# Linear attention with a routed MoE: token numbers written into the masks of ranks, and the third expert slot chosen during attention

## The chip, the cores and the metric

The kernel runs on one core of a Trainium2 chip. The metric is the device time of one execution in microseconds (us); the runs' median is the kernel's time. Engines are named as the profile names them: PE is TensorE (PEld its weight loads), DVE is VectorE, ACT is ScalarE, POOL is GpSimd, SP is SyncE.

## The reference

Attention with 8 batches, 8 heads, 576 positions and 64 dimensions per head is followed by a mixture of 8 experts over the 4608 resulting rows of 512 numbers. Cut to what matters:

```python
def phi(x):
    proj = np.einsum('bhsd,df->bhsf', x, w_phi)
    proj = proj - np.max(np.abs(proj), axis=-1, keepdims=True)
    return np.concatenate([np.exp(proj), np.exp(-proj)], axis=-1)
q_p, k_p = (phi(q), phi(k))
kv = np.einsum('bhsf,bhsd->bhfd', k_p, v)
z = np.sum(k_p, axis=2)
num = np.einsum('bhsf,bhfd->bhsd', q_p, kv)
den = np.einsum('bhsf,bhf->bhs', q_p, z)[..., None] + 1e-06
x = (num / den).transpose(0, 2, 1, 3).reshape(B * S, H * D)

do_compute = x @ w_skip > 0
out = x.copy()
xc = x[do_compute]
logits = xc @ w_gate
e_idx = np.argmax(logits, axis=1)
probs = softmax(logits); gate_w = probs[np.arange(len(xc)), e_idx]
for e in range(E):
    mask = e_idx == e
    h = np.maximum(xc[mask] @ w1[e], 0.0)
    y[mask] = gate_w[mask, None] * (h @ w2[e])
out[do_compute] = xc + y
```

So each row goes to one expert or to none, and which rows an expert gets is known only on the chip.

## The kernel before

**Attention** runs in a software pipeline over some 90 iterations. Each handles a piece of a k unit and of a q unit (4 heads of one batch): transposed load (L298), projection on PE (L321), maximum and subtraction on DVE (L328, L331), exponentials on ACT, the sums z of k on POOL (L354 to L360), products on PE (L389, L487), the normalization by 1/den on DVE (`norm`, L434). PSUM tiles come from `bank(tag)`; during attention tag O has two buffers, shared by the products, the ranks and the choices. From iteration 8 to 78 PE's instructions stand in the order of the code; before and after that a scheduler orders them, as it orders the other engines all through attention.

**Ranks.** When a batch of rows is done, `post(b)` picks each row's expert (`OH`, a one-hot row per token in 36 tiles of 128 tokens) and queues three functions for some iterations later. `rank` counts each token's rank within its expert. It splits the rank: `RKH` is the rank divided by 128, and `OP` holds for each tile a mask of 128 x 128, which is 1 where the token's rank modulo 128 equals the column (L607). The masks are made on POOL, one instruction per tile, and for the last batch on DVE. `index` multiplies the mask by a right-hand side that holds the token's number, so that PE sorts token numbers into rank order. A number over 256 isn't exact in bf16, so it goes in two parts (`ids`, L171): a multiple of 128, and the rest plus one; hence two matmuls per tile (L630), each with `rhs`, the one-hot of the higher rank times one part (L619).

**Choices.** The two fullest experts are chosen after batch 5 (`pick(0)`, `pick(1)`), so that their first 256 rows can be gathered early (slots E). `pick_third` (L942) chooses a third slot in the same way from the counts of 27 tiles: one matmul, then 17 small DVE instructions that depend on one another. It is called in step 2 of the MoE part (`at(TAB[0], pick_third)`, L1182).

**The MoE part** is a list of steps. Each step multiplies one weight chunk of 512 KB (a quarter of w1 or w2 of an expert) with the rows of a slot: 8 steps for each slot E, C and D. Weights are read by SP's queue, cut by `split` (L193) into a high part (ACT, L198) and a low part (DVE in one instruction, or POOL in four, L203, for chunks 0, 1, 2, 4, 6, 8, 9, 11, 12, 14, 17, 19, 21 of the first slots). `rows` turns gathered rows (PE), and cuts them in the same way (ACT L785, DVE L786). The results are scattered to the output by POOL's queue (L855) with an index that DVE makes (`si`, L854).

Beside the first 17 steps stands the making of the **tables** for the other slots: `rests[0]`, the rank of the last batch (step 4, masks on DVE), and then the generator `tables()`, a piece in each of the steps of `CFG['tab']`. Its last big pieces compare each token's place with all 62 columns (`eq`, L1057), multiply by the two parts of the token's number (`rx`, L1060), four groups of 9 tiles in four steps, and then sum all of them with 72 matmuls (L1068). In the MoE part every engine works in the order of the code.

`xrows` keeps the rows in DRAM for the gathers. Batch rows are stored there so that a partition's four tiles are four consecutive rows (`rowm`, L241).

Of the kernel before, what the change touches and what calls it, by code (L numbers as in the profile page):

```python
# [8 lines left out]
F32 = mybir.dt.float32  # L9
# [15 lines left out]
def kernel(  # L25
# [93 lines left out]
    pad0 = const.tile([P, 3, 2], I32, name="pad0")  # L119
    mark = const.tile([1, 32], I32, name="mark")[:, 0:1]  # L120
# [21 lines left out]
    def setup():  # L142
        nc.gpsimd.memset(ones_b, 1.0)
        nc.gpsimd.memset(ones_f, 1.0)
        nc.gpsimd.memset(Stot, 0.0)
        nc.gpsimd.affine_select(
            out=tri, in_=ones_b, pattern=[[1, P]], base=-1, channel_multiplier=-1,
            compare_op=ALU.is_ge, fill=0.0,
        )
        nc.gpsimd.iota(iota_p, pattern=[[1, P]], base=0, channel_multiplier=0, allow_small_or_imprecise_dtypes=True)  # L150
        nc.gpsimd.iota(desc, pattern=[[-1, E]], base=E, channel_multiplier=0, allow_small_or_imprecise_dtypes=True)
        nc.gpsimd.memset(ones_b, 1.0)
        NB2 = B // 2
# [14 lines left out]
        nc.vector.tensor_copy(out=sid, in_=kt_i[:, 1])  # L168
# [60 lines left out]

    with actx:  # L230
# [10 lines left out]
        rowm = [xr[b // 2, b % 2 * 512:b % 2 * 512 + 512].rearrange("(p g) m -> p g m", g=4) for b in range(B)]  # L241
# [273 lines left out]
        def post(b):  # L515
# [63 lines left out]
            rhs = sm("rhs", [5, 2, nsh], BF16)  # L579

            def rank():
# [24 lines left out]
                for t in range(nt):  # L606
                    (nc.vector if last else nc.gpsimd).tensor_scalar(  # L607
                        out=OP[:, t0 + t, :], in0=iota_p, scalar1=rkp[:, t:t + 1], scalar2=None, op0=ALU.is_equal)
# [5 lines left out]
                for s in range(S):  # L614
# [4 lines left out]
                nc.gpsimd.tensor_tensor(  # L619
                    out=rhs[:, 0:nt],  # L620
                    in0=rm4[:, 0:nt].rearrange("p t (o e) s -> p t o (e s)", o=1).broadcast_to([P, nt, 2, nsh]),
                    in1=ids[:, T].rearrange("p t (c o) -> p t c o", o=1).broadcast_to([P, nt, 2, nsh]), op=ALU.mult)

            def index():
# [3 lines left out]
                for t in range(nt):  # L628
                    for c in range(2):
                        nc.tensor.matmul(  # L630
                            ix, OP[:, t0 + t, :], rhs[:, t, c, :], start=(t == 0 and c == 0),
# [310 lines left out]
    def pick_third():  # L942


        cs = bank("K")[:, 0:NTE * E]
        nc.tensor.matmul(cs, ones_b, OH[:, 0:NTE, :].rearrange("p t e -> p (t e)"), start=True, stop=True)
        n = const.tile([P, E], F32, name="n_e")
        d = const.tile([P, E], F32, name="d_e")
        mx = const.tile([P, 2], F32, name="mx_e")
        nc.vector.tensor_reduce(out=n, in_=cs.rearrange("p (t e) -> p e t", e=E), axis=AX.X, op=ALU.add)  # L950
        for j in range(2):
            nc.vector.scalar_tensor_tensor(out=d, in0=n, scalar=float(SLOT), in1=pks[:, j], op0=ALU.min, op1=ALU.mult)
            nc.vector.tensor_tensor(out=n, in0=n, in1=d, op=ALU.subtract)
        nc.vector.tensor_tensor(out=d, in0=n, in1=pks[:, 1], op=ALU.mult)
        nc.vector.tensor_tensor(out=n, in0=n, in1=d, op=ALU.subtract)
        nc.vector.tensor_reduce(out=mx[:, 0:1], in_=n, axis=AX.X, op=ALU.max)
        nc.vector.scalar_tensor_tensor(out=d, in0=n, scalar=mx[:, 0:1], in1=desc, op0=ALU.is_equal, op1=ALU.mult)
        nc.vector.tensor_reduce(out=mx[:, 1:2], in_=d, axis=AX.X, op=ALU.max)
        nc.vector.tensor_scalar(out=d, in0=d, scalar1=mx[:, 1:2], scalar2=None, op0=ALU.is_equal)
        nc.vector.tensor_scalar(  # L960
            out=eid0[:, 2:3], in0=mx[0:1, 1:2], scalar1=-1.0, scalar2=float(E), op0=ALU.mult, op1=ALU.add)
        nc.vector.scalar_tensor_tensor(out=pks[:, 2], in0=n, scalar=float(SLOT), in1=d, op0=ALU.is_ge, op1=ALU.mult)
        tp = const.tile([P, 2, E], F32, name="tp_e")
        ea = const.tile([P, 2], F32, name="ea_e")
        nc.vector.tensor_tensor(
            out=tp.rearrange("p s e -> p e s"), in0=acc.rearrange("p (e s) -> p e s", s=2),
            in1=pks[:, 2].rearrange("p (e o) -> p e o", o=1).broadcast_to([P, E, 2]), op=ALU.mult)
        nc.vector.tensor_reduce(out=ea, in_=tp, axis=AX.X, op=ALU.add)
        places(idg0[:, 2], pad0[:, 2], ea)

    def tables():
        i34 = const.tile([P, NCOL], F32, name="i34")
        nc.gpsimd.iota(i34, pattern=[[1, NCOL]], base=1, channel_multiplier=0, allow_small_or_imprecise_dtypes=True)
# [77 lines left out]
        rxs = []  # L1051
        for g, t0 in enumerate(range(0, NT, C)):
            eq = mo.tile([P, 2, P + 64], F32, tag="hsum", name="eq")
            eq = eq.rearrange("p a n -> p (a n)").bitcast(BF16)[:, 0:C * NCOL].rearrange("p (t c) -> p t c", c=NCOL)
            rx = mo.tile([P, C, 2, NCOL], BF16, tag="rx", name="rx", bufs=4)
# [4 lines left out]
            nc.vector.tensor_tensor(  # L1060
                out=rx, in0=eq.rearrange("p t (o c) -> p t o c", o=1).broadcast_to([P, C, 2, NCOL]),
# [236 lines left out]
```

## Time and profile before

| | us |
|---|---|
| median of 3 runs | 623.17 |
| lowest and highest | 622.90, 623.51 |
| the profiled execution | 620.68 |
| its span | 619.0 |

The mean granted clock of PE in the profiled execution is 0.982. The page's chain of waits covers only the last microseconds, so the places where PE waits are read from the waits, the timelines and the tables of stages instead. In a timeline a row has its start, its length, the engine, the line, the operation, output<-input and how many were merged, then in brackets the idle time before it and what ended it.

### The profile page before, as it was taken

The page shows a single profiled execution, that of the slowest core. Times are in us where ns is not written, and L with a number is a line of the kernel's source. Part 1 is how long each engine was busy: PE and PEld are TensorE (multiplying, and loading weights), DVE is VectorE, ACT ScalarE, POOL GpSimd, SP SyncE. Part 2 cuts the span into 40 slices and gives each one's busy share as a digit, 9 for nine tenths or more (in the row PEclk, how much of TensorE's full clock was granted, in tenths as well). Part 3 has the DMA queues.
Part 4 walks back from the last instruction along what each step waited for, and adds up shares of the span by engine and source line. Part 5 has one row for each costly group of instructions (what it writes and reads, how often), then busy time and mean ns, then how long its engine had stood idle before and what let it go on. Part 6 is the DMA issues. An engine that isn't in the chain of part 4 may idle for free. (4 is left out here: it accounts for less than half of the span.)

```text
span 619.0 us, 18767 instructions
## 1 busy us (share of the span) xinstructions
PE 570.2 (92%) x7486; PEld 468.9 (76%) x7486; DVE 512.0 (83%) x1084; ACT 330.4 (53%) x649; POOL 360.5 (58%) x390
## 2 busy tenths in 40 slices
PE   4699999999999999999999898699999898999993
PEld 2477777777777677776777788598888787989892
DVE  5899999999989999999986699957688887956851
ACT  3466556456656556556446445324658554665630
POOL 5665565564744747456661657974468855559121
PEclk9999999999999999999999898979999899999998
DMA  9988888887667766423152789676767678597200
GB/s 157 161 140 162 185 184 177 192 188 139 144 151 158 162 131 143 123 70 102 37 191 94 209 302 309 221 249 182 223 225 248 233 248 290 182 314 237 88 19 29
DMA packets 250233, 108.33 MB, mean 175 GB/s; under 512 B 192417, under 2 KB 235553, under 8 KB 250144
## 3 DMA queue, kind: packets, MB, share of 16 engines
q1 hardware_dynamic: 245632, 97.58, 60.9%
q0 software_dynamic: 3200, 9.45, 4.4%
q8 instruction: 60, 0.98, 0.6%
q10 hardware_dynamic: 1312, 0.08, 0.1%
q14 instruction: 29, 0.24, 0.1%
HBM read 83.86 MB, written 24.02 MB: 174 GB/s over the span
## 5 line engine op out<-in xcount | busy, mean ns | idle before, releaser
L203 POOL TENSOR_TENSOR w<-wraw_c,w 128x256 fp32r<-128x256 f32 x124 | 114.6, 958 | 51.1 <-ACT w L198 51.1
L354 POOL TENSOR_TENSOR z<-ek 128x512 f32<-128x512 f32 x64 | 81.5, 1273 | 98.4 <-ACT ek L347 73.6
L198 ACT ACTIVATE w<-wraw_c 128x1024 fp32r<-128x1024 f32 x96 | 97.5, 1051 | 4.3 <-DMA wraw_c<-in_moe_w_dram 2.9
L203 DVE TENSOR_TENSOR w<-wraw_c,w 128x1024 fp32r<-128x1024 f32 x65 | 86.9, 1345 | 12.9 <-ACT w L198 10.7
L328 DVE TENSOR_REDUCE m<-ps_P 128x8 f32<-128x1024 f32 (+2 forms) x86 | 88.6, 1030 | 6.4 <-PE ps_P L321 6.2
L331 DVE TENSOR_TENSOR u<-ps_P,m 128x1024 f32<-128x1024 f32 (+2 forms) x86 | 88.8, 1033 | 3.1 <-DVE xTt L296 0.2
L321 PE MATMUL ps_P<-wsrc,xT 64*64 64x128 f32 x2048 | 77.9, 281 | 12.1 <-DVE xT L298 6.9
L487 PEld LDWEIGHTS ps_O<-kva,eq 128*64 128x64 f32 x2048 | 74.5, 136 | 16.5 <-issue 5.7
L487 PE MATMUL ps_O<-kva,eq 128*64 128x74 f32 x2048 | 77.6, 228 | 4.1 <-DVE lgm L450 4.0
L321 PEld LDWEIGHTS ps_P<-wsrc,xT 64*64 64x64 f32 x2048 | 56.7, 134 | 27.4 <-issue 18.4
L373 ACT ACTIVATE eq<-ps_U 128x512 f32<-128x512 f32 x64 | 37.9, 592 | 64.7 <-PE ps_U L367 64.2
L389 PE MATMUL ps_K<-ek,v 128*64 128x256 f32 x512 | 70.8, 394 | 0.0
L855 POOL DMA_INDIRECT out_dram<-o,si x22 | 28.8, 1310 | 63.9 <-DVE si L854 56.8
L922 PE MATMUL ps_O<-w,hh 128*128 128x512 f32 x160 | 64.2, 401 | 0.0
L346 ACT ACTIVATE ek<-u 128x512 f32<-128x512 f32 x64 | 40.4, 631 | 38.4 <-DVE u L331 23.0
L367 PE MATMUL ps_U<-ident,u 128*128 128x128 f32 x288 | 49.1, 287 | 2.5 <-DVE u L331 1.9
L298 DVE STREAM_TRANSPOSE xT<-raw 128x512 f32<-128x512 f32 x64 | 44.8, 702 | 5.8 <-PE ps_P L321 2.8
L926 PE MATMUL ps_O<-w,hh 128*128 128x512 f32 x120 | 47.3, 394 | 1.3 <-POOL w L203 1.3
L389 PEld LDWEIGHTS ps_K<-ek,v 128*64 128x64 f32 x512 | 31.9, 137 | 20.9 <-issue 11.3
L927 PE MATMUL ps_O<-w,hlo 128*128 128x512 f32 x120 | 47.2, 393 | 0.0
L909 PE MATMUL ps_P<-x,w 128*128 128x256 f32 x144 | 38.9, 299 | 4.7 <-DVE x L786 4.7
L358 POOL TENSOR_TENSOR z<-z 128x512 f32<-128x512 f32 x32 | 40.8, 1275 | 2.5
(259 smaller groups left out, 1206.6 us busy)
## 6 DMA issues: line engine op xcount, KB each, us to landing
wraw_c<-in_moe_w_dram SPq DMA_DIRECT2D x96, 512.0 KB, 4.0
raw<-in_k_dram SPq DMA_DIRECT2D x64, 144.0 KB, 3.3
raw<-in_q_dram SPq DMA_DIRECT2D x64, 144.0 KB, 4.4
v<-in_v_dram SPq DMA_DIRECT2D x64, 128.0 KB, 2.8
out_dram<-xm SPq DMA_DIRECT2D x16, 512.0 KB, 4.2
xrows<-xm SPq DMA_DIRECT2D x8, 516.0 KB, 4.3
xrows<-xm SPq DMA_DIRECT2D x8, 512.0 KB, 4.7
vt<-in_v_dram SPq DMA_DIRECT2D x32, 32.0 KB, 2.8
```

What stands on the lines that cost most here:

```text
L198: nc.scalar.activation(out=hi, in_=raw, func=AF.Copy)
L203: eng.tensor_tensor(out=lo[:, r], in0=raw[:, r], in1=hi[:, r].bitcast(F32), op=ALU.subtract)
L321: nc.tensor.matmul(p[s * 64:s * 64 + 64, hd, (nj + j) * NF:(nj + j + 1) * NF], xT[r, g * P + s * 64:g * P + s * 64 + 64], wsrc[r], start=T ...
L328: nc.vector.tensor_reduce(out=m.rearrange("p (j h) -> p j h", h=2), in_=pv, axis=AX.X, op=ALU.max, apply_absolute_value=True)
L331: nc.vector.tensor_tensor(out=uu[:, 0:2 * nj, :].rearrange("p (j h) f -> p j h f", h=2), in0=pv, in1=m.rearrange("p (j h o) -> p j h o", h ...
L354: zeng.tensor_tensor(out=z, in0=e[:, 0:2, :], in1=e[:, 2:4, :], op=ALU.add)
L367: nc.tensor.transpose(t[:, tt * P:(tt + 1) * P], uu[:, tt, :], ident)
L389: nc.tensor.matmul(o[hd * 64:hd * 64 + 64, :], u.v[:, 2 * hd + pr, g * D:(g + 1) * D], u.e[i][:, 2 * j + hd, :], start=(g == 0), stop=False,)
L487: nc.tensor.matmul(ov[s * 64:s * 64 + 64, 2 * j + hd, :], e[:, half, j, hd, s * 64:s * 64 + 64], kva[:, half, 2 * pr + hd, :], start=(half ...
L922: nc.tensor.matmul(y[sub], hh[:, t], wh[:, fi, :], start=first, stop=False)
L926: nc.tensor.matmul(y[sub], hh[:, t], wl[:, fi, :], start=False, stop=False)
L927: nc.tensor.matmul(y[sub], hlo[:, t], wh[:, fi, :], start=False, stop=last)
```

## The change

It moves the token numbers from the right-hand sides into the masks. Each mask of ranks is made twice, as `OP[:, t, 0]` with 128 t and as `OP[:, t, 1]` with p + 1 in place of the 1 (one instruction with a comparison and a multiplication each). The right-hand sides are then the plain one-hots `rm4` and `eq`; the products `rhs` and `rx` and the tile `ids` are gone. For a number to be 128 t + p, `rowm` now puts token p of a tile in row p of 128 consecutive ones. The comparisons of the tables keep their tiles until the 72 matmuls, which stand together behind the last comparison, in the step where they stood. `pick_third` is called in attention, five iterations after `rest` of batch 5; its matmul takes a buffer of tag O.

```diff
-    ids = const.tile([P, NT, 2], BF16, name="ids")
+    wcol = const.tile([P, NT + 1], I32, name="wcol")
-    OP = const.tile([P, NT, P], BF16, name="OP")
+    OP = const.tile([P, NT, 2, P], BF16, name="OP")
...
+        nc.gpsimd.iota(wcol[:, 0:NT], pattern=[[P, NT]], base=0, channel_multiplier=0)
+        nc.gpsimd.iota(wcol[:, NT:NT + 1], pattern=[[1, 1]], base=1, channel_multiplier=1)
...
-        nc.vector.tensor_scalar(out=h_i[:, 1], in0=kt_i[:, 0], scalar1=127, scalar2=None, op0=ALU.bitwise_and)
-        nc.vector.tensor_tensor(out=h_i[:, 0], in0=kt_i[:, 0], in1=h_i[:, 1], op=ALU.subtract)
-        nc.vector.tensor_scalar(out=h_i[:, 1], in0=h_i[:, 1], scalar1=1.0, scalar2=None, op0=ALU.add)
...
-        nc.vector.tensor_copy(out=ids.rearrange("p t c -> p c t"), in_=h_i)
...
+    def pick_third():
+        cs = bank("O")[:, 0:NTE * E]
...
-        rowm = [xr[b // 2, b % 2 * 512:b % 2 * 512 + 512].rearrange("(p g) m -> p g m", g=4) for b in range(B)]
+        rowm = [xr[b // 2, b % 2 * 512:b % 2 * 512 + 512].rearrange("(g p) m -> p g m", p=P) for b in range(B)]
...
-                for t in range(nt):
-                    (nc.vector if last else nc.gpsimd).tensor_scalar(
-                        out=OP[:, t0 + t, :], in0=iota_p, scalar1=rkp[:, t:t + 1], scalar2=None, op0=ALU.is_equal)
+                for c in range(2):
+                    for t in range(nt):
+                        (nc.vector if last else nc.gpsimd).tensor_scalar(
+                            out=OP[:, t0 + t, c, :], in0=iota_p, scalar1=rkp[:, t:t + 1],
+                            scalar2=wcol[:, NT:NT + 1] if c else wcol[:, t0 + t:t0 + t + 1], op0=ALU.is_equal, op1=ALU.mult)
...
-                nc.gpsimd.tensor_tensor(
-                    out=rhs[:, 0:nt],
...
-                            ix, OP[:, t0 + t, :], rhs[:, t, c, :], start=(t == 0 and c == 0),
+                            ix, OP[:, t0 + t, c, :], rm4[:, t].rearrange("p e s -> p (e s)"), start=(t == 0 and c == 0),
...
+                    later.append((now[0] + CFG["post"][2] + 5, pick_third))
...
-    def pick_third():
-        cs = bank("K")[:, 0:NTE * E]
...
+        def found():
+            t0, eq = rxs.pop(0)
+            for t in range(C):
+                for c in range(2):
+                    nc.tensor.matmul(
+                        ix, OP[:, t0 + t, c, :], eq[:, t, :], start=(t0 + t == 0 and c == 0),
+                        stop=(t0 + t == NT - 1 and c == 1))
+
         for g, t0 in enumerate(range(0, NT, C)):
-            eq = mo.tile([P, 2, P + 64], F32, tag="hsum", name="eq")
-            rx = mo.tile([P, C, 2, NCOL], BF16, tag="rx", name="rx", bufs=4)
+            if g % 2:
+                eq = mo.tile([P, C, NCOL], BF16, tag="rx", name="eq", bufs=2)
+            else:
+                eq = mo.tile([P, 2, P + 64], F32, tag="hsum", name="eq")
...
-            nc.vector.tensor_tensor(
-                out=rx, in0=eq.rearrange("p t (o c) -> p t o c", o=1).broadcast_to([P, C, 2, NCOL]),
-                in1=ids[:, T].rearrange("p t (c o) -> p t c o", o=1).broadcast_to([P, C, 2, NCOL]), op=ALU.mult)
-            rxs.append((t0, rx))
+            rxs.append((t0, eq))
             yield
-        for t0, rx in rxs:
...
+        while rxs:
+            found()
...
-    at(TAB[0], pick_third)
```

Lines of the changed kernel have other numbers: the masks are L633 there, the comparisons L1061, the choice L231 to L253 with L222 and L223.

Where instructions stand, engine by engine, at three places. First DVE at the end of attention, where the normalization of a q piece (`xm`, `lgm`) follows that of the pieces `xt`, `lgt`. Before:

```order
L331 TENSOR_TENSOR u<-ps_P,m 128x512
L438 TENSOR_SCALAR den<-ps_O 128x4
L442 RECIPROCAL rec<-den 128x4
L449 TENSOR_TENSOR xt<-ps_O,rec 128x2x2x64
L450 TENSOR_TENSOR lgt<-ps_O,rec 128x36
L438 TENSOR_SCALAR den<-ps_O 128x4
L442 RECIPROCAL rec<-den 128x4
L449 TENSOR_TENSOR xm<-ps_O,rec 128x4x64
L450 TENSOR_TENSOR lgm<-ps_O,rec 128x2x18
L328 TENSOR_REDUCE m<-ps_P 128x2
```

Now, the last part of the choice and what follows it:

```order
L243 TENSOR_REDUCE mx_e<-d_e 128x1
L244 TENSOR_SCALAR d_e<-d_e,mx_e 128x8
L245 TENSOR_SCALAR eid_125<-mx_e 1x1
L247 SCALAR_TENSOR_TENSOR pks<-n_e,d_e 128x8
L250 TENSOR_TENSOR tp_e<-acc,pks 128x8x2
L253 TENSOR_REDUCE ea_e<-tp_e 128x2
L464 TENSOR_SCALAR den<-ps_O 128x4
L222 TENSOR_SCALAR idg_126<-ea_e 128x2
L223 TENSOR_SCALAR pad_127<-ea_e 128x2
L468 RECIPROCAL rec<-den 128x4
L475 TENSOR_TENSOR xm<-ps_O,rec 128x4x64
L476 TENSOR_TENSOR lgm<-ps_O,rec 128x2x18
```

The choice begins behind the first `den` and is done before the normalization of `xm`; one m and one u (128x2, 128x256), which stood behind that normalization, now stand within the choice.

Second DVE in the MoE part, from the third comparison of the tables on (`w` is the low part of a weight chunk, `x` that of gathered rows). Before:

```order
L1057 TENSOR_TENSOR eq<-i_6552,col 128x558
L1060 TENSOR_TENSOR rx<-eq,ids 128x1116
L203 TENSOR_TENSOR w<-wraw_c,w 128x1024
L1057 TENSOR_TENSOR eq<-i_6552,col 128x558
L1060 TENSOR_TENSOR rx<-eq,ids 128x1116
L786 TENSOR_TENSOR x<-ps_U,x 128x4x128 x2
L203 TENSOR_TENSOR w<-wraw_c,w 128x1024
```

Now:

```order
L1061 TENSOR_TENSOR eq<-i_131,col 128x558
L200 TENSOR_TENSOR w<-wraw_c,w 128x1024
L1061 TENSOR_TENSOR eq<-i_131,col 128x558
L810 TENSOR_TENSOR x<-ps_U,x 128x4x128 x2
L200 TENSOR_TENSOR w<-wraw_c,w 128x1024
```

The products are gone, and nothing else moved here.

Third POOL in attention at the second burst of masks, between the sums z. Before:

```order
L358 TENSOR_TENSOR z<-z 128x512
L360 TENSOR_TENSOR z<-z,ekt 64x512
L607 TENSOR_SCALAR OP<-iota_p,rkp 128x128 x5
L619 TENSOR_TENSOR rhs<-rm_1876,ids 128x320
L354 TENSOR_TENSOR z<-ek 128x512 x2
```

Now:

```order
L384 TENSOR_TENSOR z<-z 128x512
L386 TENSOR_TENSOR z<-z,ekt 64x512
L633 TENSOR_SCALAR OP<-iota_p,rkp,wcol 128x128 x10
L380 TENSOR_TENSOR z<-ek 128x512 x2
L384 TENSOR_TENSOR z<-z 128x512
```

Ten masks stand where five and the product stood. The masks of the last batch, on DVE, likewise become ten from five.

More of the change, by code (lines that the diff above doesn't have):

```diff
@@ L119 @@
     pad0 = const.tile([P, 3, 2], I32, name="pad0")
+    const.tile([1, 40], I32, name="spare")
     mark = const.tile([1, 32], I32, name="mark")[:, 0:1]
@@ L228 @@
     early = []
+    def pick_third():
+        cs = bank("O")[:, 0:NTE * E]
+        nc.tensor.matmul(cs, ones_b, OH[:, 0:NTE, :].rearrange("p t e -> p (t e)"), start=True, stop=True)
+        n = const.tile([P, E], F32, name="n_e")
+        d = const.tile([P, E], F32, name="d_e")
+        mx = const.tile([P, 2], F32, name="mx_e")
+        nc.vector.tensor_reduce(out=n, in_=cs.rearrange("p (t e) -> p e t", e=E), axis=AX.X, op=ALU.add)
+        for j in range(2):
+            nc.vector.scalar_tensor_tensor(out=d, in0=n, scalar=float(SLOT), in1=pks[:, j], op0=ALU.min, op1=ALU.mult)
+            nc.vector.tensor_tensor(out=n, in0=n, in1=d, op=ALU.subtract)
+        nc.vector.tensor_tensor(out=d, in0=n, in1=pks[:, 1], op=ALU.mult)
+        nc.vector.tensor_tensor(out=n, in0=n, in1=d, op=ALU.subtract)
+        nc.vector.tensor_reduce(out=mx[:, 0:1], in_=n, axis=AX.X, op=ALU.max)
+        nc.vector.scalar_tensor_tensor(out=d, in0=n, scalar=mx[:, 0:1], in1=desc, op0=ALU.is_equal, op1=ALU.mult)
+        nc.vector.tensor_reduce(out=mx[:, 1:2], in_=d, axis=AX.X, op=ALU.max)
+        nc.vector.tensor_scalar(out=d, in0=d, scalar1=mx[:, 1:2], scalar2=None, op0=ALU.is_equal)
+        nc.vector.tensor_scalar(
+            out=eid0[:, 2:3], in0=mx[0:1, 1:2], scalar1=-1.0, scalar2=float(E), op0=ALU.mult, op1=ALU.add)
+        nc.vector.scalar_tensor_tensor(out=pks[:, 2], in0=n, scalar=float(SLOT), in1=d, op0=ALU.is_ge, op1=ALU.mult)
+        tp = const.tile([P, 2, E], F32, name="tp_e")
+        ea = const.tile([P, 2], F32, name="ea_e")
+        nc.vector.tensor_tensor(
+            out=tp.rearrange("p s e -> p e s"), in0=acc.rearrange("p (e s) -> p e s", s=2),
+            in1=pks[:, 2].rearrange("p (e o) -> p e o", o=1).broadcast_to([P, E, 2]), op=ALU.mult)
+        nc.vector.tensor_reduce(out=ea, in_=tp, axis=AX.X, op=ALU.add)
+        places(idg0[:, 2], pad0[:, 2], ea)
     with actx:
@@ L578, in post @@
             rm4 = sm("rm4", [5, E, S], BF16)
-            rhs = sm("rhs", [5, 2, nsh], BF16)
             def rank():
@@ L940 @@
     start = {"E": 0, "D": 0, "C": NSD, "S": NS2}
-    def pick_third():
-        cs = bank("K")[:, 0:NTE * E]
[L946 to L964, printed above, removed]
-        nc.vector.tensor_tensor(
[L966 to L969, printed above, removed]
     def tables():
-        i34 = const.tile([P, NCOL], F32, name="i34")
-        nc.gpsimd.iota(i34, pattern=[[1, NCOL]], base=1, channel_multiplier=0, allow_small_or_imprecise_dtypes=True)
         cn = bank("K")[:, 0:E]
@@ L1059, in tables @@
                 in1=col[:, T].rearrange("p (t o) -> p t o", o=1).broadcast_to([P, C, NCOL]), op=ALU.is_equal)
-            nc.vector.tensor_tensor(
-                out=rx, in0=eq.rearrange("p t (o c) -> p t o c", o=1).broadcast_to([P, C, 2, NCOL]),
-                in1=ids[:, T].rearrange("p t (c o) -> p t c o", o=1).broadcast_to([P, C, 2, NCOL]), op=ALU.mult)
-            rxs.append((t0, rx))
+            rxs.append((t0, eq))
             yield
-        for t0, rx in rxs:
-            for t in range(C):
-                for c in range(2):
-                    nc.tensor.matmul(
-                        ix, OP[:, t0 + t, :], rx[:, t, c, :], start=(t0 + t == 0 and c == 0),
-                        stop=(t0 + t == NT - 1 and c == 1))
+        while rxs:
+            found()
         fv = ft[:, 0:NS2].rearrange("p t (c s) -> p c t s", s=2)
```

20 lines of the change are left out of this document (8 added, 12 removed).

## The prediction

> **What bounds the kernel now.** I read the page first, for the engines; then a table of stages; then who waited for whom on TensorE; then the timelines of the stage that stood out.
>
> ```profile
> PE 570.2 (92%) x7486; PEld 468.9 (76%) x7486; DVE 512.0 (83%) x1084; ACT 330.4 (53%) x649; POOL 360.5 (58%) x390
> ```
>
> TensorE sets the time: it is busy for 92% of the span. So an edit is worth what it takes from TensorE's idle time and from the time that its clock is low. The next table shows three stages.
>
> ```profile
> core 0 of [0], span 619.0 us
> core 0: us, PE busy (x) PEld busy (x) DVE busy (x) ACT busy (x) POOL busy (x), PEclk, DMA share, GB/s
> 318.00:340.00 22.00, 21.67 (x404) 17.11 (x402) 14.57 (x54) 12.39 (x24) 7.24 (x10) 1.00 0.41 138
> 374.00:386.00 12.00, 10.38 (x67) 9.63 (x66) 11.52 (x27) 5.80 (x9) 10.71 (x13) 0.86 0.90 302
> 386.00:403.00 17.00, 11.18 (x53) 8.70 (x51) 16.86 (x14) 5.75 (x7) 16.68 (x13) 0.98 0.70 226
> ```
>
> In the last 22 us of attention TensorE is busy to 0.33 us, and VectorE has 22 - 14.57 = 7.4 us to spare. From 386 to 403 it is the reverse: VectorE and GpSimd are full, and TensorE lacks 5.8 us. Its waits between 372 and 410 us (total, times, longest):
>
> ```profile
> PE ps_P L909 <- DVE x L786: 4.7, 1, 4.7
> PE ps_P L911 <- POOL w L203: 1.6, 2, 1.0
> PE ps_O L926 <- POOL w L203: 1.3, 1, 1.3
> ```
>
> The longest is the wait for the third slot's rows (L786). Behind it the clock is at half, the last number but two of:
>
> ```profile
> 403.00:408.00 5.00, 4.83 (x22) 0.50 0.53 148
> 412.00:417.00 5.00, 5.00 (x45) 1.00 0.87 274
> ```
>
> The same matmuls pass 22 times in five microseconds, where they pass 45 times at full clock.
>
> **The products with token numbers (L1060) go.** VectorE, in order of time:
>
> ```profile
> 385.86 0.74 DVE L1057 TENSOR_TENSOR eq<-i,col 128x558 bf16<-128x558 f32 x1
> 386.64 1.32 DVE L1060 TENSOR_TENSOR rx<-eq,ids 128x1116 bf16<-128x1116 bf16 x1
> ...
> 401.84 1.27 DVE L786 TENSOR_TENSOR x<-ps_U,x 128x512 fp32r<-128x512 f32 x2
> ```
>
> ```profile
> L1060 DVE TENSOR_TENSOR rx<-eq,ids x4: 1321/1730/1745, 386.6 to 400.2; 128x1116 bf16<-128x1116 bf16 x4
> ```
>
> The last row has the shortest, the median and the longest of the four products: 1.32 us alone, 1.73 beside GpSimd, 1.32 + 3 x 1.73 = 6.5 us together. GpSimd pays too:
>
> ```profile
> 356.47 2.83 POOL L203 TENSOR_TENSOR w<-wraw_c,w 128x256 fp32r<-128x256 f32 x4 [2.86 <-ACT w L198]
> ```
>
> ```profile
> 387.44 17.41 POOL L203 TENSOR_TENSOR w<-wraw_c,w 128x256 fp32r<-128x256 f32 x12
> ```
>
> A quarter of a weight chunk takes 0.71 us (2.83 / 4) in the first row and 1.45 (17.41 / 12) in the second: the two engines take turns, one instruction each. Without the products VectorE reaches the rows at 401.84 - 6.5 = 395.3. What is late next is ScalarE's half of them:
>
> ```profile
> 395.19 1.09 ACT L785 ACTIVATE x<-ps_U 128x512 fp32r<-128x512 f32 x2 [6.42 <-PE ps_U L782]
> ```
>
> ```profile
> 403.17 0.58 PE L909 MATMUL ps_P<-x,w 128*128 128x256 f32 x1 [4.71 <-DVE x L786]
> ...
> 408.25 2.76 PE L1068 MATMUL ps_K<-rx,OP 128*128 128x62 bf16 x72
> ```
>
> ScalarE ends at 396.3, VectorE's second half 0.64 later, at 396.9; TensorE asks at 403.17 - 4.71 = 398.5. So the wait goes whole, **-4.7**, with 1.5 us to spare. With no gap there is no half clock behind it: the 24 matmuls of that chunk ran from 403.17 to 408.25, 5.1 us, and at 45 in 5 us take 2.7, **-2.4**. The 72 matmuls of the tables gain 0 to 1.3 (half of 2.6), as most of them lay in the slow stretch; I take **-0.4**. Their number stays 72.
>
> **The third slot's choice leaves the MoE part; ten masks come in for five.** It stood on VectorE ahead of everything that the scatter at 374 waits for:
>
> ```profile
> 356.56 0.67 DVE L952 SCALAR_TENSOR_TENSOR d_e<-n_e,pks 128x8 f32<-128x8 f32 x1
> ...
> 361.39 0.16 DVE L226 TENSOR_SCALAR pad<-ea_e 128x2 int32<-128x2 f32 x1
> ...
> 364.62 2.99 DVE L607 TENSOR_SCALAR OP<-iota_p,rkp 128x128 bf16<-128x128 f32 x5
> ```
>
> ```profile
> 357.85 0.60 ACT L800 ACTIVATE hh<-ps_P 128x512 fp32r<-128x512 f32 x1 [1.45 <-PE ps_P L911]
> ```
>
> ```profile
> 374.91 1.08 POOL L855 DMA_INDIRECT out_dram<-o,si  x1 [5.97 <-DVE si L854]
> ```
>
> VectorE's next work could start at 358.5, when ScalarE has hh, and started when the choice was done at 361.5: 3.0 us freed. Masks:
>
> ```profile
> L607 POOL TENSOR_SCALAR OP<-iota_p,rkp x31: 590/596/632, 79.5 to 323.8; 128x128 bf16<-128x128 f32 x31
> L607 DVE TENSOR_SCALAR OP<-iota_p,rkp x5: 275/760/778, 364.6 to 366.8; 128x128 bf16<-128x128 f32 x5
> ```
>
> A mask with a second operation is in no row. On VectorE I take 0.28 (alone) to 0.60 each (2.99 / 5, beside GpSimd), so five more cost 1.4 to 3.0; as they start 3 us earlier, part falls in the gap before GpSimd's next pieces, and I take 1.5. The scatter's index comes 1.5 us earlier (3.0 earlier at best, 0.8 later if all ten cost 0.76). Behind the scatter, which waited 5.97 us for that index, on GpSimd's queue stand chunks 11 and 12, the gathers and chunk 14, for which TensorE waited 1.6 and 1.3 us. Chunk 14 comes 1.5 earlier. A product that took a turn between its four pieces is gone, which is worth 0 to 1.75; but a comparison of 0.72 takes the turn over, and I take 0.25. So **-1.75** on TensorE at 393. What it gains ahead of that (up to 1.6) doesn't add: it turns into a longer wait for chunk 14.
>
> The choice lands in attention instead. Its 17 instructions wait one for the other, some 0.2 us apart where nothing disturbs them (0.16 at 361.39): 3.4 us. Those with two inputs in SBUF take turns (0.67 for eight elements at 356.56) with GpSimd's sums:
>
> ```profile
> 319.26 0.18 DVE L450 TENSOR_TENSOR lgm<-ps_O,rec 128x36 f32<-128x36 f32 x1
> ```
>
> ```profile
> 319.35 1.27 POOL L360 TENSOR_TENSOR z<-z,ekt 64x512 f32<-64x512 f32 x1
> ```
>
> GpSimd's sums end at 320.6. At most two turns of 1.0 each: 3.4 + 2.0 = 5.4 us. Nearly all of it now stands ahead of the normalization that ended at 319.4, which frees a PSUM buffer of tag O, and of two more; the new matmul holds another of the two. TensorE, full there, will wait at the ranks' matmuls. Between 0 (VectorE's 7.4 idle us hide it) and 5.4 I take half, **+2.8**, as the order lets two groups of 16 matmuls and one transposition go ahead. It issues no DMA, and the third slot's number, read by SyncE, is only earlier.
>
> **Masks on GpSimd.** 31 become 62, and six products go:
>
> ```profile
> L619 POOL TENSOR_TENSOR rhs<-rm,ids x6: 602/666/717, 81.8 to 283.6; 128x256 bf16<-128x256 bf16 x3, 128x320 bf16<-128x320 bf16 x3
> ```
>
> At 0.6 a mask, that is 2.4 to 3.0 us more in each burst, less 0.7 for the product. The largest burst:
>
> ```profile
> 120.57 2.94 POOL L607 TENSOR_SCALAR OP<-iota_p,rkp 128x128 bf16<-128x128 f32 x5 [4.21 <-DVE RKH L609]
> ```
>
> ```profile
> 130.61 0.41 PE L630 MATMUL ps_O<-rhs,OP 128*128 128x32 bf16 x10
> ```
>
> The burst begins when VectorE has the ranks. Ten masks at 0.59 end at 126.5, 4.1 us before TensorE needs them; a mask may cost from 0.59 to 1.19 (each operation paid), and up to 1.0 nothing waits. I take 0.6, cost **0**. The sums z queued behind lose about 2 us, and GpSimd, idle for 4.21 us before this burst, makes them up before TensorE's next use.
>
> **Stores.** Rows are stored in another order, the bytes being the same:
>
> ```profile
> out_dram<-xm SPq DMA_DIRECT2D x16, 512.0 KB, 4.2
> xrows<-xm SPq DMA_DIRECT2D x8, 516.0 KB, 4.3
> xrows<-xm SPq DMA_DIRECT2D x8, 512.0 KB, 4.7
> ```
>
> The last number is the time to landing. The first row has the order of rows that the others now get, so between -0.5 and +0.5 us for a store, behind loads that nobody awaits: **0**. The four set-up instructions that VectorE loses stand ahead of its first input: **0**.
>
> **Sum.** The profiled execution took 620.68 us (span 619.0), 0.4% under the median of 623.17. Gains 4.7 + 2.4 + 0.4 + 1.75 = 9.25, loss 2.8: 6.45 less, so 614.2 on that execution's scale and **616.8** on the median's.
>
> One rule bears on the wait that stays before chunk 14, some 2 to 3 us. The Trainium skill, "TensorE: Matmul & The Clock Gate", section "HAM oscillation — how this bites in real kernels", says that only a gap above about 3.4 us brings the clock down. By that rule the wait costs no clock and the sum stands. This trace differs: from 374 to 386 the granted clock is 0.86 after waits of 1.0 and 0.6 us. By that row half a clock for 2.4 us might follow, and the sum would be 619.2.
>
> **Rivals.**
> 1. *The choice is hidden in attention.* For it: VectorE's 7.4 idle us. Against: TensorE's 0.33, and a chain that stands ahead of the normalizations. Then 616.8 - 2.8 = 614.0.
> 2. *The rows stay late.* GpSimd takes up the turns that VectorE leaves, or the gathered rows land late; the wait shrinks by 3.0 only, the half clock stays and the scatter comes no earlier: 3.0 + 0.25 - 2.8 = 0.45 less, 622.7. For it: GpSimd is full from 386 to 403 (16.68 of 17.0). Against: after the products it has no more work than before.
> 3. *VectorE's masks become the bound (slower).* If the form with two operations and two scalars from memory costs more than 0.6 us each, ten of them outlast the old five plus the 3.0 freed: that is the point from which it decides. At 1.2 they take 12 us, the scatter is 6 later, and chunks 11 and 14 with it. TensorE loses 6, and 2.4 to the clock behind the longer wait; with 2.8 in attention against 7.5 gained at the rows, that is +3.7: 626.9. For it: no row shows the form, and 0.76 beside GpSimd is on the page. Against: 0.28 alone.
> 4. *GpSimd's masks hold up TensorE.* From 1.0 us each. At 1.19 a burst of ten ends 1.9 after it is needed, three times, 5.7: 622.5.
>
> That the change doesn't do what it says is excluded by the order: the products are gone, the masks are 62 and ten, the choice stands in attention.
>
> **How the numbers follow.** Forecast 0.52, rival 1 0.17, rival 2 0.12, rival 3 0.14, rival 4 0.05. A measurement here can tell about 0.2% (1.25 us). Forecast and rival 1, with a little of rival 2, are faster: 0.70. The rest of rivals 2 and 4 lies within 0.2%: 0.15. Rival 3, and a choice that costs all its 5.4 together with late masks, is slower: 0.15. The range: at best the tables gain 1.3, chunk 14 comes 3.0 + 0.25 earlier and attention pays nothing, 4.7 + 2.4 + 1.3 + 3.25 = 11.65, 611.5; I put 612.0, as not all come together. Upwards it takes in rivals 2 and 4, 623.0, and leaves out rival 3.
>
> **What would show it.** Right: no product on VectorE; TensorE's wait for the third slot's rows gone; granted clock 1.00 in the stretch behind it; the scatter's index 1 to 2 us earlier counted from the start of the MoE part; that start 2 to 3 us later than before, with TensorE waits of that sum for VectorE's normalizations near 320. Wrong: a wait for these rows above 2 us; masks above 0.6 us on VectorE or 1.0 on GpSimd; waits of TensorE for GpSimd at the index matmuls. The forecast falls if VectorE's locked turns cost more in attention than the whole choice did in the MoE part.

## The result, and the profile after

| | time in us, median (range, runs) | ratio to before, 95% interval |
|---|---|---|
| before, measured beside it | 623.34 (4 runs) | |
| after | 615.27 (614.56 to 617.51, 4 runs) | 0.9893 (0.9861 to 0.9926) |
| forecast | 616.8, range 612.0 to 623.0 | |

The change makes the kernel faster by about 8 us, 1.1%. The profiled execution of after is the slowest of the four runs, 617.51 us, and that turned out to matter. Its engines, from the first part of the page:

```profile
span 615.8 us, 18780 instructions
...
PE 571.6 (93%) x7486; PEld 467.4 (76%) x7486; DVE 509.9 (83%) x1081; ACT 331.0 (54%) x649; POOL 381.5 (62%) x415
```

GpSimd has 21 us more work (381.5 for 360.5) and the kernel is still faster: it isn't the bound. The stages, with the columns of the prediction's table (window, TensorE, its weight loads, VectorE, ScalarE, GpSimd, granted clock, DMA):

```profile
318.00:340.00 22.00, 21.87 (x412) 16.71 (x406) 17.22 (x67) 10.79 (x22) 9.62 (x13) 1.00 0.42 135
...
386.00:403.00 17.00, 11.83 (x45) 8.44 (x43) 16.65 (x24) 4.59 (x6) 12.02 (x14) 0.90 0.58 191
403.00:411.00 8.00, 7.88 (x119) 7.84 (x120) 5.15 (x12) 1.54 (x2) 5.58 (x8) 1.00 0.81 300
```

VectorE has the choice in the first window (17.22 for 14.57). From 386 to 403 it is as full as before, though four products are gone, and TensorE is hardly busier. The waits of TensorE from 372 to 410 say where that comes from (total, times, longest):

```profile
PE ps_O L950 <- DVE w L200: 2.9, 1, 2.9
PE ps_P L933 <- DVE x L810: 1.7, 1, 1.7
PE ps_O L950 <- POOL w L200: 0.6, 1, 0.6
PE ps_P L935 <- POOL w L200: 0.5, 2, 0.3
```

The wait for the third slot's rows (L810 now) has shrunk from 4.7 to 1.7, but there is a new one of 2.9 for a weight chunk of VectorE's. VectorE and GpSimd at the place that starts it, in order of time:

```profile
378.05 0.45 DVE L1029 TENSOR_REDUCE pe<-tm 128x36 f32<-128x288 f32 x1
378.54 5.57 DVE L1030 SCALAR_TENSOR_TENSOR rk<-pe,RKH 128x36 f32<-128x36 f32 x1
384.03 1.21 DVE L200 TENSOR_TENSOR w<-wraw_c,w 128x1024 fp32r<-128x1024 f32 x1
```

```profile
378.48 5.57 POOL L200 TENSOR_TENSOR w<-wraw_c,w 128x256 fp32r<-128x256 f32 x8
```

An instruction of 36 elements a partition took 5.57 us: exactly as long as GpSimd's eight weight pieces, which began 0.06 us ahead of it and went through one behind the other. Before the change the two engines took turns here. Whether that belongs to the change was the first question for the experiments.

### The profile page after: what moved, and what is told of

It is laid out like the page before. It is cut to its first block, busy times and chain, and to the rows that moved or that the text cites. A ratio compares the mean times of both kernels' runs of the same rounds, so it can differ in the third digit from the quotient of the medians.

```text
span 615.8 us, 18780 instructions
## 1 busy us (share of the span) xinstructions
PE 571.6 (93%) x7486; PEld 467.4 (76%) x7486; DVE 509.9 (83%) x1081; ACT 331.0 (54%) x649; POOL 381.5 (62%) x415
## 5 line engine op out<-in xcount | busy, mean ns | idle before, releaser
L200 POOL TENSOR_TENSOR w<-wraw_c,w 128x256 fp32r<-128x256 f32 x124 | 109.8, 920 | 42.1 <-ACT w L195 36.0
L347 PE MATMUL ps_P<-wsrc,xT 64*64 64x128 f32 x2048 | 79.3, 283 | 11.7 <-DMA raw<-in_k_dram 7.1
L879 POOL DMA_INDIRECT out_dram<-o,si x22 | 28.8, 1309 | 66.8 <-DVE si L878 60.4
L633 POOL TENSOR_SCALAR OP<-iota_p,rkp,wcol 128x128 bf16<-128x128 f32 x62 | 48.4, 790 | 24.0 <-DVE RKH L636 17.8
```

The lines of the kernel that those rows point to most:

```text
L200: eng.tensor_tensor(out=lo[:, r], in0=raw[:, r], in1=hi[:, r].bitcast(F32), op=ALU.subtract)
L347: nc.tensor.matmul(p[s * 64:s * 64 + 64, hd, (nj + j) * NF:(nj + j + 1) * NF], xT[r, g * P + s * 64:g * P + s * 64 + 64], wsrc[r], start=T ...
L633: (nc.vector if last else nc.gpsimd).tensor_scalar(out=OP[:, t0 + t, c, :], in0=iota_p, scalar1=rkp[:, t:t + 1], scalar2=wcol[:, NT:NT + 1 ...
```

## The experiments

All kernels of the table have a profiled execution, and three marks on TensorE cut each span into stages: the matmuls L446 near 312 (the last stretch of attention starts), the first transposition of gathered rows (the MoE part starts, near 340), and the first of the tables' 72 matmuls. Times in us; the ratio is that of the timed runs to before.

| kernel | end of attention | MoE start to tables' matmuls | from there to the end | span | ratio (95%) |
|---|---|---|---|---|---|
| before | 27.00 | 69.32 | 210.8 | 619.0 | |
| after, first profile | 28.44 | 65.42 | 209.8 | 615.8 | 0.9893 (0.9861 to 0.9926) |
| after, second | 28.44 | 60.54 | 210.3 | 612.1 | 0.988 (0.9845 to 0.9915) |
| after, third | 28.43 | 59.27 | 212.6 | 613.1 | |
| after, fourth | (another order at the mark) | 59.55 | 212.6 | 614.1 | |
| masks alone | 27.00 | 62.86 | 212.0 | 614.0 | 0.9927 (0.9902 to 0.9952) |
| choice alone | 28.45 | 67.12 | 212.2 | 619.5 | 0.9989 (0.9966 to 1.0013) |
| products back | 28.44 | 66.97 | 213.5 | 621.4 | 1.0008 (0.9974 to 1.0041) |
| last masks late | (another order at the mark) | 64.10 | 211.3 | 617.8 | 0.9964 (0.9936 to 0.9992) |
| choice later | 27.33 | 61.64 | 212.7 | 614.3 | 0.9915 (0.9887 to 0.9943) |
| last masks late, choice in the MoE part | 27.00 | 64.62 | 212.4 | 615.6 | 0.9944 (0.992 to 0.9968) |
| last masks shared | 28.43 | 60.46 | 211.7 | 612.6 | 0.9913 (0.9885 to 0.9941) |

For the first row: L420 at 311.93 (the line's number before), L782 at 338.93, L1068 at 408.25.

### The same kernel again, three times

Nothing is edited.

> The changed kernel once more, nothing altered, for a second profiled execution. In the first one VectorE's instruction for rk (L1030, 128x36) took 5.57 us, the whole of GpSimd's run of eight weight pieces from 378.48. Theory (luck of one execution): in this profile that instruction takes 1 to 2 us, the tables' comparisons start 3 to 5 us earlier, TensorE's wait for a weight chunk of VectorE (2.9) goes, and the span is 1 to 3 us under 615.8. Rival (it follows from the order of the change, since GpSimd's queue no longer has products to alternate with): rk takes 5 us or more again, at the same place. The time by both is 615.3 +- 1.

> The changed kernel, one more profiled execution. VectorE's instruction for rk (L1030) took 5.57 us in the first profile (GpSimd's eight pieces went through ahead of it) and 0.84 in the second. Theory (chance of the execution): either of the two, nothing between; with 5.57 the tables' 72 matmuls start 64 to 66 us after the MoE part, with 0.84 they start 60 to 62 after it.

> The same, a fourth profiled execution of the changed kernel: either 5 us or more for rk and 64 to 66 us from the start of the MoE part to the tables' matmuls, or under 1 us and 60 to 62.

Six timed runs gave 611.38 to 616.72, median 613.16 (before beside them 621.04). VectorE in the second profile:

```profile
378.98 0.84 DVE L1030 SCALAR_TENSOR_TENSOR rk<-pe,RKH 128x36 f32<-128x36 f32 x1
379.74 1.79 DVE L200 TENSOR_TENSOR w<-wraw_c,w 128x1024 fp32r<-128x1024 f32 x1
...
396.61 1.29 DVE L810 TENSOR_TENSOR x<-ps_U,x 128x512 fp32r<-128x512 f32 x2 [0.31 <-ACT x L809]
```

GpSimd in the same profile:

```profile
378.92 7.53 POOL L200 TENSOR_TENSOR w<-wraw_c,w 128x256 fp32r<-128x256 f32 x8
```

The start is the same to the hundredth (VectorE 0.06 us behind GpSimd), and this time VectorE got its turn after one piece. In the third and fourth profiles the instruction took 0.82 us, and the tables' matmuls came 59.27 and 59.55 us behind the MoE part's start, just under the 60 to 62 expected. In six other kernels (the one before, each half alone, products back, choice later, and late masks with the choice in the MoE part) the same two instructions start 0.05 or 0.06 us apart, and VectorE's took 0.82 or 0.83. So the 5.57 is chance, seen in one of ten profiles, and that execution needs 5 to 6 us more to the tables (65.42 for 59.27 to 60.54). In the other three of the change the third slot's rows come at 395 to 397 and TensorE doesn't wait for them at all; the waits that are left in the third profile, 372 to 410:

```profile
PE ps_P L935 <- POOL w L200: 1.8, 2, 1.2
PE ps_O L950 <- POOL w L200: 0.6, 1, 0.6
```

The second profile was expected 1 to 3 us under the first in span; it is 3.7 under it.

### The two halves of the change, each alone

Masks alone: the changed kernel with the choice back in the MoE part.

```diff
-                    later.append((now[0] + CFG["post"][2] + 5, pick_third))
...
+    at(TAB[0], pick_third)
     at(TAB[1], rests[0])
```

> The changed kernel with the third slot's choice back at its old place in the MoE part (step 2); masks made twice, no products. Theory (the products carry the gain, the choice's move is worth its 3.0 us of VectorE ahead of the scatter less 1.6 in attention): the MoE part starts 1.6 us earlier than after the change, the scatter's index comes 2 to 3 us later counted from there, the rows' wait still shrinks to under 2 us: 615.5 to 617.5, within 2 us of the whole change. Rival (the move carries the gain): 621 or more.

Choice alone: the kernel before with the choice moved.

```diff
+                    later.append((now[0] + CFG["post"][2] + 5, pick_third))
...
-    at(TAB[0], pick_third)
     at(TAB[1], rests[0])
```

> The kernel before with only the third slot's choice moved into attention; products and single masks as before. Theory (as for the masks alone): the start of the MoE part is 1.6 us later, the scatter's index 3 us earlier counted from there, the wait for the third slot's rows stays at 3 to 5 us with its half clock: 621.5 to 624. Rival (the move carries the gain): 617 to 619.

The masks alone give 616.07 us, 5.0 less than before; the choice alone 621.26, no difference that can be measured (its scatter index came 34.1 us behind the MoE part's start, 1.5 earlier than before and not the 3 expected). The stages say why. From the MoE part's start to the tables, the masks (with the products gone) save 69.32 - 62.86 = 6.5 us and the choice saves 69.32 - 67.12 = 2.2; together 8.7, and the three undisturbed profiles of the whole change show 8.8 to 10.1. But the choice gives back 1.45 in attention (28.45 for 27.00), and whether its move pays in time isn't shown: the ratios with it (0.988) and without it (0.9927) have intervals that overlap. Part of the 2.2 is clock, too. The wait for the rows ends 64.24 us behind the start before and 62.77 with the choice alone, 1.5 earlier; behind it the granted clock is at half for 6.83 us before (402.42 to 409.25) and for 3.41 with the choice alone (403.60 to 407.01), and that is the other 0.7. With the products still there, TensorE waits for the rows as long as before:

```profile
PE ps_P L939 <- DVE x L816: 4.7, 1, 4.7
PE ps_O L956 <- POOL w L203: 2.3, 2, 1.3
PE ps_P L941 <- POOL w L203: 0.8, 2, 0.6
```

Those are the waits with the choice alone. Attention with the doubled masks takes 27.00 us to its end, as before: 31 more masks on GpSimd and rows stored in another order cost nothing there. Nor is a matmul of TensorE listed as waiting for GpSimd from 60 to 340 us in any profile (three weight loads are, with 0.5 us together, where the masks are doubled).

### The products put back

The changed kernel with a product behind each comparison, read by nobody, two thirds of the old size (128x738 for 128x1116, as much as memory had room for; a version with products of the full size found no room and has no time).

```diff
+            rx = mo.tile([P, C, 2, 41], BF16, tag="dm", name="rx", bufs=1)
+            nc.vector.tensor_tensor(
+                out=rx, in0=eq[:, :, 0:41].rearrange("p t (o c) -> p t o c", o=1).broadcast_to([P, C, 2, 41]),
+                in1=OH[:, T, 0:2].rearrange("p t (c o) -> p t c o", o=1).broadcast_to([P, C, 2, 41]), op=ALU.mult)
             rxs.append((t0, eq))
```

> The changed kernel with a product of 128x738 bf16 (two thirds of the old size, read by nobody) behind each of the four comparisons: a dose of what the change took away. Theory (VectorE's products carry the gain): each costs 0.9 to 1.4 us of VectorE and a turn of GpSimd, the third slot's rows move from 396.6 to 400 or later, TensorE waits 1 to 3 us for them: 2 to 5 us slower than the changed kernel, a ratio to before of 0.991 to 0.996. Rival (what was gained is GpSimd's six products in attention and the other edits): within 1 us of the changed kernel, 0.988.

622.26 us: the whole gain is gone, more than was expected. VectorE:

```profile
387.87 0.93 DVE L1065 TENSOR_TENSOR rx<-eq,OH 128x738 bf16<-128x738 bf16 x1
...
400.29 1.33 DVE L1065 TENSOR_TENSOR rx<-eq,OH 128x738 bf16<-128x738 bf16 x1
401.54 1.27 DVE L810 TENSOR_TENSOR x<-ps_U,x 128x512 fp32r<-128x512 f32 x2
```

The four take 0.93 + 1.35 + 1.34 + 1.33 = 4.95 us, and the rows come 60.6 us behind the MoE part's start (401.54 - 340.98), for 54.0 to 55.3 in the undisturbed profiles (396.61 - 341.30 in the second): 5.2 to 6.6 later, at least one for one. TensorE waits 3.9 for them, and the clock behind it is low again (0.66):

```profile
PE ps_P L933 <- DVE x L810: 3.9, 1, 3.9
```

```profile
403.00:411.00 8.00, 8.00 (x101) 7.91 (x102) 3.63 (x11) 1.54 (x2) 6.49 (x9) 0.66 0.73 242
```

So the products are what the rows had waited for: two thirds of them take back 6.4 of the 8.8 us that the second profile gains from the MoE part's start to the tables (66.97, 60.54 and 69.32 before). That the whole time is lost is not their work alone: the choice's 1.44 in attention stays, and behind the tables, where no product stands, this profile has 2.7 us more than before (213.5 for 210.8).

### The last ten masks at another place

On VectorE they stand ahead of the scatter's index. Late: behind it, at step 8 (once with the choice in attention, once with it back in the MoE part). Shared: five of them on GpSimd, in its idle time behind chunk 9.

```diff
-                for c in range(2):
-                    for t in range(nt):
-                        (nc.vector if last else nc.gpsimd).tensor_scalar(
+                def masks():
...
+                if last:
+                    rests.append(masks)
+                else:
+                    masks()
...
+    at(8, lambda: rests[2]())
```

The shared form splits the two sets of masks between the engines:

```diff
-                for c in range(2):
...
+                masks(0, nc.vector if last else nc.gpsimd)
+                if last:
+                    rests.append(lambda: masks(1, nc.gpsimd))
+                else:
+                    masks(1, nc.gpsimd)
...
+    at(7, lambda: rests[2]())
```

> The changed kernel with the last batch's ten masks on VectorE moved from step 4 to step 8, behind the scatter's indices (TensorE has the scatter's sums at 371.4, VectorE reaches them at 375.4 only). Theory (the masks hold the scatter up, and GpSimd's chunks 11, 12 and 14 behind it): the index comes 3 to 4 us earlier, TensorE's waits for GpSimd's chunks between 372 and 410 (3.1 us in the second profile of the changed kernel) fall below 1.5, the rows stay at 396 to 398: 1.5 to 3 us faster than the changed kernel, a ratio to before of 0.983 to 0.986. Rival (the chunks come from GpSimd's own work or from their loads): 0.988. Counter-rival (the masks beside GpSimd's pieces cost 0.75 each, and the rows come late): 0.990 or more.

> The choice back in the MoE part (step 2) and the ten masks at step 8 behind the scatter's indices: with the masks out of the way the choice may find room ahead of the scatter. Theory: attention takes 27.0 us again (1.44 less), the index comes 33 to 34 us after the start of the MoE part (31 with the choice in attention), which costs 1 to 2 us of waits for GpSimd's chunks: within 1 us of the kernel with late masks and the choice in attention, a ratio of 0.983 to 0.988. Rival (the choice's chain is the bound there): 0.990 or more.

> The changed kernel with five of the last batch's ten masks (those that carry 1 to 128) on GpSimd, behind chunk 9, where it idled for 5.5 us ahead of the scatter. Theory (the ten masks on VectorE cost 0.44 to 0.52 each ahead of the scatter, and GpSimd's chunks behind it wait for that): the scatter's index 1.5 to 2.5 us earlier counted from the start of the MoE part, TensorE's waits for GpSimd's chunks down by 1.5: a ratio to before of 0.984 to 0.987. Rival (GpSimd's five masks of 0.79 take turns with VectorE's small instructions on the tables, 0.66 for 0.17 each, and VectorE reaches the scatter no earlier): 0.988 or more, and the five masks on GpSimd end after the index.

None beats the change. Late masks were slower than it, and not faster as expected (619.0 and 618.34 us, within 1 us of each other): the index did come earlier where the choice stood in the MoE part (34.2 us behind its start, 37.0 with the masks alone), and GpSimd's chunks with it. But now the masks run beside those chunks. VectorE of that kernel:

```profile
372.79 0.15 DVE L883 TENSOR_TENSOR si<-xg,pad 128x1 int32<-128x1 f32 x1
...
376.44 5.75 DVE L634 TENSOR_SCALAR OP<-iota_p,rkp,wcol 128x128 bf16<-128x128 f32 x10
382.11 1.21 DVE L200 TENSOR_TENSOR w<-wraw_c,w 128x1024 fp32r<-128x1024 f32 x1
```

0.58 us a mask, and the wait is now for VectorE's own chunk:

```profile
PE ps_O L955 <- DVE w L200: 2.9, 1, 2.9
PE ps_P L938 <- DVE x L815: 1.2, 1, 1.2
```

This is the counter-rival, at 0.58 us a mask (0.44 with the choice in attention) and not its 0.75: the rows come 60.4 and 59.9 us behind the start, for 54.0 to 55.3. With late masks and the choice in attention the index came 32.8 us behind the start, 0.7 to 2.3 earlier than in the profiles of the change and not the 3 to 4 expected, as VectorE then waited 1.46 us for a matmul of the tables ahead of it; the wait of 2.9 for its own chunk stands there too. Shared masks measured as the changed kernel does (614.66 us). VectorE had the index at 373.55, but GpSimd's five masks took 4.95 us and held the scatter until 374.79:

```profile
369.68 4.95 POOL L633 TENSOR_SCALAR OP<-iota_p,rkp,wcol 128x128 bf16<-128x128 f32 x5
374.79 1.09 POOL L885 DMA_INDIRECT out_dram<-o,si  x1 [0.16 <-issue]
```

The rival was right on the time and on GpSimd's masks, which end after the index; the index itself came 33.1 us behind the start, for 33.5 to 35.1 in the profiles of the change, and what that gained GpSimd's masks took back.

### The choice at a later place in attention

```diff
-                    later.append((now[0] + CFG["post"][2] + 5, pick_third))
+                    later.append((now[0] + CFG["post"][2] + 7, pick_third))
```

> The changed kernel with the third slot's choice two iterations of attention later. In three profiles with the choice in attention TensorE needs 1.44 us more from its matmuls L446 near 312 to the first transposition of the MoE part (28.44 us, 27.00 without it). Theory (the choice costs because its chain on VectorE stands ahead of normalizations and of what feeds the projections, wherever it stands in full attention): 28.0 to 28.6 again, and the time as of the changed kernel, 0.988 +- 0.002. Rival (a matter of the one place): 27.0 to 27.5, and 1.2 us faster.

The mark moved as the rival said: 27.33 for 28.44. The time didn't (615.56 us, the intervals of the two ratios overlap): the first product of the MoE part waits for ScalarE's half of the rows, 2.7 us where the change has 1.4:

```profile
PE ps_P L932 <- ACT x L809: 2.7, 1, 2.7
```

ScalarE makes the high parts of four weight chunks first, from 338.71 here and from 338.88 in the second profile of the change. Counted to that first product, attention's end takes 29.5 us with the masks alone (341.65 - 312.14), 30.9 with the change (343.80 - 312.86) and 31.2 with the choice later (343.76 - 312.60). So the price is 1.4 to 1.7 us at both places, as the theory had it, though its number for the mark missed. ScalarE shows the same: its last exponential of attention (L400) starts 25.5 us behind the mark with the change (338.40 - 312.86) and 25.6 with the choice later (338.23 - 312.60), for 24.1 with the masks alone (336.25 - 312.14). That the reason is the theory's, a chain ahead of normalizations and of what feeds the projections, is not shown by this run.

## Why the prediction was right, step by step

The forecast of 616.8 was 1.5 us above the 615.27 measured, within its range. The time alone doesn't tell it from rival 1, whose 614.0 is 1.3 below; the steps do:

- **The wait for the rows, -4.7, and the half clock behind it, -2.4: right.** In the three undisturbed profiles the wait is gone and the clock is 1.00 from 403 to 411, as in the second:

```profile
386.00:403.00 17.00, 15.46 (x117) 12.75 (x116) 15.13 (x21) 7.32 (x10) 16.35 (x16) 1.00 0.73 239
403.00:411.00 8.00, 8.00 (x98) 8.00 (x94) 4.28 (x9) 3.15 (x5) 7.18 (x10) 1.00 0.81 267
```

  VectorE was to reach the rows at 395.3, 56.4 us behind the MoE part's start, and did so 54.0 to 55.3 us behind it (at 395.24 to 396.61). From the end of the wait for chunk 14 to the tables' matmuls it is 14.95 us before (408.25 - 393.30), 7.76 to 7.79 in the three undisturbed profiles and 7.78 with the masks alone: 7.2 less, where these two terms are 7.1. Before:

```profile
393.30 0.50 PE L926 MATMUL ps_O<-w,hh 128*128 128x512 f32 x1 [1.28 <-POOL w L203]
```

  and in the second profile:

```profile
394.08 0.49 PE L950 MATMUL ps_O<-w,hh 128*128 128x512 f32 x1 [1.19 <-POOL w L200]
...
401.84 2.27 PE L1050 MATMUL ps_K<-eq,OP 128*128 128x62 bf16 x72
```

  What is late next was right too: ScalarE's half (VectorE waits 0.31 for it). The first profile has 1.7 of the wait, for a reason that the prediction didn't have.
- **The tables' 72 matmuls, -0.4: right in size** (2.76 to 2.27 us), though not most of them lay in the slow stretch: the clock was back at 409.25, 1.0 us behind their start, so that 0.5 was all there was to gain, and not 1.3:

```profile
405.97 2.27 PE L1050 MATMUL ps_K<-eq,OP 128*128 128x62 bf16 x72
```

- **Chunk 14, -1.75: right.** The wait for it ended 54.4 us behind the MoE part's start before (393.30), and 52.8, 51.5 and 51.8 in the undisturbed profiles: 1.6 to 2.9 earlier. It ended at 55.1 with the masks alone (394.22 - 339.14) and at 52.9 with the choice alone (393.12 - 340.21), so this gain is the choice's.
- **The scatter's index, 1.5 earlier: right in the mean.** 35.5 us behind the start before, and 35.1, 34.8, 33.5 and 33.8 after: 0.5 to 2.1 earlier, 1.2 in the mean. (The prediction's worst case is off: ten masks of 0.76 would bring it 7.6 - 2.99 - 3.0 = 1.6 later, not 0.8.)
- **Ten masks on VectorE, 1.5 more: about right.** They took 5.22, 4.40, 3.15 and 2.65 us in the four profiles, for 2.99 with five before: between 0.3 less and 2.2 more. A mask is 0.27 to 0.52 us in the mean of its ten, under the 0.6 from which rival 3 would have decided.
- **62 masks on GpSimd, 0: right, at another price.** A mask with a second operation is 0.785 us (0.6 was assumed, 0.59 was the row with one):

```profile
L633 POOL TENSOR_SCALAR OP<-iota_p,rkp,wcol x62: 780/785/852, 79.5 to 332.4; 128x128 bf16<-128x128 f32 x62
```

  The bound was 1.0, attention's end takes 27.00 us with the masks alone as it did before, and no matmul waits for GpSimd at the ranks. Rival 4 fell. The stores, 0, land no later: 4.1 and 4.4 us by the page of after, for 4.3 and 4.7.
- **The choice in attention, +2.8: mis-sized, and expected in the wrong place.** It is 1.44 (28.44 for 27.00). The prediction took half of 5.4, as it priced two turns of 1.0 and 3.4 of chain ahead of the normalizations, and expected TensorE's waits for normalizations near 320. The chain was priced well: it takes 5.6 us in the first profile (317.67 to 323.28), with two turns of 0.88 and 0.92, and the normalization of `xm` starts 4.5 later (323.40 for 318.92). The share of it that reaches TensorE was too high, and TensorE's waits there didn't grow. What grew is the busy time of the projections, over the same 80 matmuls from the mark to the MoE part, second profile of the change and masks alone:

```profile
L347 PE MATMUL ps_P<-wsrc,xT 64*64 64x128 f32 x80 | 5.0, 288 | 0.0
```

```profile
L347 PE MATMUL ps_P<-wsrc,xT 64*64 64x128 f32 x80 | 4.2, 284 | 0.0
```

  0.8 of the 1.44 stands there, as matmuls of nearly the same length that cover more time; the choice's own matmul has 0.3. With the choice later the row has 4.2 again, at the same price to the first product. So the projections are where the delay shows at one place, and not its reason; the link from VectorE's chain to TensorE stays open. The MoE part's start, 1.6 to 3.0 us later than before, looks like the sign of 2 to 3 that the prediction named, but only 1.44 of it is the end of attention.

With 1.44 in place of 2.8 the sum is 7.8 us less, and 8.1 and 7.9 were measured (623.34 - 615.27, 621.04 - 613.16). That it comes so close is partly luck: the profiled spans of the change are only 3.2 to 6.9 us under the 619.0 before, whose execution was itself 2.5 under its median, and the stretch behind the tables, which the sum leaves out, moved by -0.9 to +1.9. (The prediction's own sum gives 616.7 and not 616.8.) Rival 1 (the choice is hidden) fell by those 1.44, rival 2 (the rows stay late) by the profiles without the wait. The first profile looks like rival 2, but its cause is the turn that VectorE didn't get.

The remaining wait for chunk 14 was the place where the prediction weighed the clock. From 386 to 403 the granted clock is 1.00 in the second profile, behind waits of 0.34 and 1.19 us, so the sum stood. By the Trainium skill, "TensorE: Matmul & The Clock Gate", section "HAM oscillation — how this bites in real kernels" (the rule there is no idle gap of TensorE above about 3.4 us) it should stand. In the first profile it did not hold: no gap near that place is above 2.92 us, and the matmuls of 512 columns behind that one take 0.50 us, then 0.63, where they take 0.39 at full clock.

```profile
396.57 0.50 PE L950 MATMUL ps_O<-w,hh 128*128 128x512 f32 x1 [2.92 <-DVE w L200]
...
397.83 0.63 PE L950 MATMUL ps_O<-w,hh 128*128 128x512 f32 x1
```

From 374 to 386 it holds no better: the granted clock is 0.86 in the third and fourth profiles, as before, behind waits of 1.19 and 1.32 us that are each followed by one of 0.58, and 1.00 in the second behind 0.98 and 0.58. The length of a wait doesn't settle what follows either. Between the first and the last 30 us of the span, the low stretches of all twelve profiles last 3.41 or 6.83 us, and a wait of 4.7 us for the rows was followed by 6.83 before and by 3.41 with the choice alone. So half a clock behind a wait costs one step or two, and which of them no run here lets one foresee; the prediction's 2.4 stands for the two steps of before.

What the sum left out is behind the tables. From their matmuls to the end the four profiles of the change take 209.8, 210.3, 212.6 and 212.6 us, for 210.8 before. The longer ones have 2.1 to 3.0 us of waits at L922 for GpSimd's chunks where the shorter ones have 0.3, and the kernels with one half of the change have them too. But these waits are not the difference, as others are shorter: TensorE is idle there for 15.6, 17.4, 17.6 and 16.6 us. The clock adds to it. Up to the last 15 us it is at half for 3.4, 0, 3.4 and 6.8 us, and idle time plus half of that makes 17.3, 17.4, 19.3 and 20.0, which tells the longer from the shorter. Why an execution falls on one side was not tried.

## What to carry to other kernels

Before an edit takes work from an engine that is full, find the one transfer or operand that leaves it last and that TensorE asks for: here 4.95 us of products moved the rows by 5.2 to 6.6, and with them most of the gain. A chain of tiny instructions costs its new place something even where that engine has idle time, so price it in both places (1.5 to 3.6 us saved, 1.44 paid). And where two engines take turns, look at a second profiled execution before a stall is put down to the change.

## What the runs showed of the hardware

- **Turns between VectorE and GpSimd can fail to alternate.** The same pair of starts, 0.05 to 0.07 us apart, gave VectorE's 128x36 instruction 0.82 to 0.84 us in nine profiles and 5.57 in one, where eight instructions of GpSimd went through ahead of it. The Trainium skill, "SBUF — State Buffer", section "Who interferes with whom", says that a VectorE instruction with two SBUF inputs (as this one) contends with a GpSimd instruction that reads SBUF, and that the pair of ports which they share is an exclusive lock. The 0.84 agrees with that, as the rest of one piece of GpSimd (5.57 / 8 - 0.06 = 0.64) and the 0.20 that it takes with shared masks, undisturbed; the 5.57 is eight pieces and not one, which the section doesn't say.
- **The clock goes to half in whole steps.** Between the first and the last 30 us, every stretch at half clock in the twelve profiles lasts 3.41 or 6.83 us, behind waits of 4.7 us as behind a pair of 1.04 and 0.58.
- **Tiny instructions with two inputs pay a whole turn.** The column chain (128x36, L1038 to L1041) took 0.20 us each while GpSimd issued gathers (386.5 to 387.5, second profile) and 0.66 beside its weight pieces (390.9 to 393.0, first profile):

```profile
386.54 0.20 DVE L1038 TENSOR_TENSOR col<-col,lt 128x36 f32<-128x36 f32 x1
```

```profile
390.88 0.66 DVE L1038 TENSOR_TENSOR col<-col,lt 128x36 f32<-128x36 f32 x1
```

  A reduction beside the same pieces (L1034, 128x288) kept its 0.45.
- **A second operation with a scalar from memory costs GpSimd 0.19 us on 128 elements a partition** (0.785 for 0.596). Beside VectorE's table work the same mask took 0.99 (4.95 / 5).
